# Two decode attentions on one core: A's second heads scored on the VectorE, one softmax step for four heads, and a gather dealt to 64 partitions

## The chip, the core and the metric

The kernel runs on one core of a Trainium2 chip: TensorE (PE), VectorE (DVE), ScalarE (ACT), GpSimd (POOL), a queue processor for transfers (SP), and 16 DMA engines. The metric is device time in microseconds (us), as the median of the runs.

## What is computed

One token `x` (448 numbers) goes through two attention blocks over cached keys and values, and a gate mixes the two results. Block A has 16 heads with a cache each; block B has 16 query heads on 8 caches, two heads to a cache.

```python
g = sigmoid((x * gate_w).sum(-1))
# A: H = 16; B: Hq = 16 on Hkv = 8;  Sk = 8192, Dh = 256, D = 448, all float32
q = (x @ wq).reshape(heads, Dh)
p = softmax(q @ k_cache^T * Dh ** -0.5)       # over 8192 keys, per head
o = p @ v_cache
block = o.reshape(heads * Dh) @ wo
out = g * block_A + (1 - g) * block_B
```

Every key and value is used once (in B for two heads), so some 430 MB are read for little arithmetic.

## The kernel before

**Sets and units.** The work is cut into eight sets (`NS`). Set `s` holds three units `(s, r)`: unit 2 is one B cache with its two heads, units 0 and 1 are two A heads. `UNITS = [2, 0, 1]` is their order. Each unit has four tiles (`NT`) of 2048 keys: a K tile and a V tile of 128 x 4096 numbers each. There are 96 tiles in all; the V tile of a step comes three steps (`LEAD`) after its K tile.

**The stream.** The host lays everything out in the order of use: K, V, query weights (`wq`), output weights (`wo`). `plan()` cuts this into 54 loads of up to 15,872 numbers per partition, and SP issues them one after another into a ring of three slots. A load can be issued when everything in the load three before it has been used. The last loads are cut finer; the last V tile comes in three pieces, and the last output weights come behind it in six.

**Scores.** In most units the PE multiplies K by the query (`scores`); DVE takes a minimum, ACT takes the exponential, DVE transposes it to weights `pr`. Units in `BY_ROW` go another way (`scores_by_row`): DVE multiplies the K tile in its slot by the query laid out over all partitions (`qa`), and reduces each row of 256 numbers to a score. Of a set's three units, before, only unit 0 is in `BY_ROW`. The PE then does `attend`: weights times V, summed over a unit's four tiles into the PSUM tile `o`. `take` folds that into `ob`.

**Softmax over tiles.** Each tile has its own minimum and sum (`st`). `gather(u)` lays them out in `gs`, `combine(u)` sums them on the PE and turns them into weights on one partition (`ew`, `es`, `z`, `wr`), `column(u)` turns them into a column `sel` by a PE product with `ones`, and `project_o(u)` multiplies `ob` by `sel`, into `ocs`. `emit_set` and `emit` multiply that by the output weights into `Y`. These steps are put off by `wait(n, f)`, which runs `f` after `n` more ticks; every finished K tile is a tick, and at the end the V tiles of the last three steps are.

**The gather by indirect DMA.** Set 4's query weights come partly by an indirect DMA that POOL issues (`side`). Only the partitions in `SIDE_ROWS` receive a row; `SIDE_SHARE` says how many of each group of eight partitions do. So the gather can put more bytes on some DMA engines than on others, while the stream loses the same weights on all partitions alike.

**Order on the engines.** The kernel is recorded once in program order (`Seq`), each engine executes its instructions in that order, and waits are derived from what overlaps. Nothing is reordered, so what is written earlier stands ahead in its engine's queue. The profile puts nearly all instructions at line 149, where they are emitted; they're told apart by their tiles.

Of the kernel before, what the change touches and what calls it, by code (L numbers as in the profile page):

```python
# [3 lines left out]
F32 = mybir.dt.float32  # L4
BF16 = mybir.dt.bfloat16
AF = mybir.ActivationFunctionType
OP = mybir.AluOpType
# [194 lines left out]
BY_ROW = {(s, 0) for s in range(NS)}  # L202
# [7 lines left out]
SIDE_SHARE = {0: 8, 2: 8, 7: 8, 8: 8, 15: 8, 4: 7, 1: 5, 3: 1, 6: 1, 10: 1}  # L210
# [3 lines left out]
SB, SA = 2 * DH, 64  # L214
# [56 lines left out]
def gated_decode_attention_kernel(  # L271
# [23 lines left out]
    zero = const.tile([P, P], BF16, name="zero")  # L295
# [29 lines left out]
    rows4 = const.tile([P, 4], F32, name="rows4")  # L325
# [6 lines left out]
    in4 = const.tile([P, 2, NG], F32, name="in4")  # L332
    nc.vector.tensor_copy(in4[:, 0, :], rows4)
# [6 lines left out]
    cols = const.tile([P, NT, NG, NT], F32, name="cols")  # L340
    nc.vector.memset(cols, 0.0)
    for t in range(NT):
        nc.vector.tensor_copy(cols[:, t, :, t], in4[:, 1, :])

    spread32 = const.tile([2 * BLK, P], F32, name="spread32")
    nc.vector.memset(spread32, 0.0)
    nc.vector.memset(spread32[BLK:BLK + 1, :], 1.0)

    QB = {}
    for par in range(2):  # L350
        for r in (r for r in range(3) if (par, r) not in BY_ROW or (par + 2, r) not in BY_ROW):
            QB[par, r] = const.tile([P, 2, 64], F32, name=f"qb{par}{r}")
            nc.vector.memset(QB[par, r], 0.0)

    xz = const.tile([P, KF + 2, BLK], F32, name="xz")
    nc.vector.memset(xz, 0.0)
# [15 lines left out]
    gate = const.tile([1, 2], F32, name="gate")  # L374

    def clear(t, n):
        nc.tensor.matmul(t[:, :n], zero, zero[:, None, :n // 4].to_broadcast([P, 4, n // 4]), start=True, stop=False, skip_group_check=True)
# [10 lines left out]
    def prepare(gw):  # L388
        clear(YY[0], D)
        gp = ps_s.tile([1, 1], F32, name="sm")  # L390
        for c in range(KF + 1):
            nc.tensor.matmul(gp, xz[:, c, 0:1], gw[:, c:c + 1], start=(c == 0), stop=(c == KF))
# [3 lines left out]
        nc.vector.reciprocal(gate[:, 0:1], ge)  # L396
        nc.vector.tensor_scalar(gate[:, 1:2], gate[:, 0:1], -1.0, 1.0, op0=OP.mult, op1=OP.add)
# [5 lines left out]
    def project(s, c0, w):  # L403

        if c0 == 0:
            QR[s] = ps_s.tile([2 * BLK, 2 * DH], F32, name="sm")
        q = QR[s]
        for j in range(w.shape[1]):
            a, c = divmod(c0 + j, KF)
            for a in (a,) if a < 2 else (0, 1):  # L410
                c = c if c0 + j < 2 * KF else KF
                nc.tensor.matmul(q[BLK * a:BLK * (a + 1), :], xz[:, c if c < KF else KF + a, :], w[:, j, :],
                                 start=(c == 0), stop=(c == KF), skip_group_check=True)
        if c0 + w.shape[1] == 2 * KF + 1:
            copy_out(s, q)
# [5 lines left out]
    def project_side(s, view, far):  # L421

        q = ps_s.tile([2 * BLK, 2 * DH], F32, name="sm")
        near = view[:, :KF * SREST].rearrange("p (c n) -> p c n", c=KF)
        rest = view[:, KF * SREST:]
        for a in range(2):
            nc.tensor.matmul(q[BLK * a:BLK * (a + 1), :], xz[:, KF + a, :], rest, start=True, stop=False,
                             skip_group_check=True)
        for c in range(KF):
            nc.tensor.matmul(q[BLK:2 * BLK, SA:], xz[:, c, :], near[:, c, :], start=False, stop=(c == KF - 1),  # L430
                             skip_group_check=True)
        for c in range(SC8):
            at = c * (SB + SA)
            nc.tensor.matmul(q[0:1, :], x8[:, c:c + 1], far[:, at:at + SB], start=False, stop=(c == SC8 - 1),
                             skip_group_check=True)
            nc.tensor.matmul(q[BLK:BLK + 1, :SA], x8[:, c:c + 1], far[:, at + SB:at + SB + SA], start=False,
                             stop=(c == SC8 - 1), skip_group_check=True)
        copy_out(s, q)

    def spread(s):  # L440
# [7 lines left out]
        for r, a, h, M in ((2, 0, 0, 2), (0, 1, 0, 1), (1, 1, 1, 1)):  # L448
            if (s, r) in BY_ROW:
                qa = ps_s.tile([P, DH], F32, name="sm")  # L450
                nc.tensor.matmul(qa, spread32, qr[:, h * DH:(h + 1) * DH], start=True, stop=True)
                QA[s, r] = small.tile([P, DH], F32, name="qa", bufs=1)
                nc.scalar.activation(QA[s, r], qa, AF.Copy, scale=-scale)
                continue
            nc.vector.tensor_scalar(QB[s % 2, r][:, :, BLK:BLK + M], qt[:, h:h + M, :, a].rearrange("p h e -> p e h"),
                                    -scale, None, op0=OP.mult)

    def scores(u, t, j0, kt):
# [6 lines left out]
        qb = QB[u[0] % 2, u[1]]  # L465
# [13 lines left out]
        pr = small.tile([P, NB * BLK], F32, name="pr", bufs=LEAD + 2)  # L479
# [5 lines left out]
    def scores_by_row(u, t, j0, kt):  # L485
# [10 lines left out]
        if j0 + n < ROWS:  # L496
# [9 lines left out]
        pr = small.tile([P, NB * BLK], F32, name="pr", bufs=LEAD + 2)[:, :ROWS * NG * NT].rearrange(  # L506
            "p (q c k) -> p q c k", c=NG * NT, k=2)
# [25 lines left out]
    def gather(u):  # L533

        M = heads(u)
        GS[u] = small.tile([P, 2, NG, NT, M], F32, name=f"gs{M}")
        st = ST[u][:, :, None, :].to_broadcast([P, 2, NG, NT])
        if u in BY_ROW:
            nc.vector.tensor_tensor(GS[u][:, :, :, :, 0], st, in4[:, :, :, None].to_broadcast([P, 2, NG, NT]), op=OP.mult)
        elif M == 1:  # L540
            nc.vector.tensor_tensor(GS[u][:, :, :, :, 0], st, POS[M][:, None].to_broadcast([P, 2, NG, NT]), op=OP.mult)
        else:
            pos = POS[M].rearrange("p g (t m) -> p g t m", m=M)
            for k in range(2):
                nc.vector.tensor_tensor(GS[u][:, k], ST[u][:, k, None, :, None].to_broadcast([P, NG, NT, M]), pos, op=OP.mult)

    def combine(u):

        M = heads(u)
        n = NG * NT  # L550
        gi = 1 if u[1] == 2 else 0
        T = ps_s.tile([1, 2, n * M], F32, name="sm")
        nc.tensor.matmul(T, ones, GS[u].rearrange("p k g t m -> p k (g t m)"), start=True, stop=True)
        mn = small.tile([1, 2], F32, name="mnr")
        z = small.tile([1, 2], F32, name="z")
        ew = small.tile([1, 2 * n], F32, name="ew")[:, :n * M]
        es = small.tile([1, 2 * n], F32, name="es")[:, :n * M]
        nc.vector.tensor_reduce(mn[:, :M], T[:, 0, :].rearrange("p (c m) -> p m c", m=M), axis=AX.X, op=OP.min)
        for m in range(M):
            nc.scalar.activation(ew[:, m::M], T[:, 0, m::M], AF.Exp, bias=mn[:, m:m + 1], scale=-1.0)  # L560
        nc.vector.tensor_tensor(es, ew, T[:, 1, :], op=OP.mult)
        nc.vector.tensor_reduce(z[:, :M], es.rearrange("p (c m) -> p m c", m=M), axis=AX.X, op=OP.add)
        rz = small.tile([1, 2], F32, name="rz")
        nc.vector.reciprocal(rz[:, :M], z[:, :M])
        WR[u] = small.tile([1, NG // M, n, M, 2], F32, name="wr")
        for m in range(M):
            nc.vector.tensor_scalar(
                WR[u][:, :, :, m, :], ew[:, None, m::M, None].to_broadcast([1, NG // M, n, 2]),
                rz[:, m:m + 1], gate[:, gi:gi + 1], op0=OP.mult, op1=OP.mult)

    def column(u):
        M = heads(u)
        cl = ps_s.tile([P, 1], F32, name="sm")
        nc.tensor.matmul(cl, WR.pop(u).rearrange("p c x m k -> p (c x m k)"), ones[:1, :], start=True, stop=True)
        SEL[u] = small.tile([P, 2], F32, name="sel")
        if M == 2:
            nc.vector.tensor_scalar(SEL[u], which, cl, None, op0=OP.mult)
        else:
            nc.scalar.activation(SEL[u][:, :1], cl, AF.Copy)

    def project_o(u):
        M = heads(u)
        oc = ps_s.tile([P, 2, 2], F32, name="sm")
        for e in range(2):
            nc.tensor.matmul(oc[:, e, :M], OB[u][:, e::2], SEL[u][:, :M], start=True, stop=True)
# [48 lines left out]
    def piece(kind, i, at, view):  # L634
# [17 lines left out]
        elif kind == "k":  # L652
# [54 lines left out]
    ys = const.tile([P, YN], F32, name="ys")  # L707
# [90 lines left out]
```

## Time and profile before

| what | before |
| --- | --- |
| median of 3 runs | 1005.64 us (1005.63 to 1005.69) |
| profiled execution | 1005.52 us, of it span 1003.6 us |
| PE busy | 586.4 us (58%) |
| DVE busy | 459.6 us (46%) |
| ACT busy | 94.1 us (9%) |
| stream, share of 16 DMA engines | 99.4%, 431.14 MB |
| gather | 0.89 MB |
| read from HBM | 433.20 MB, 432 GB/s over the span |
| mean granted TensorE clock | 0.774 |

A group's row gives engine, operation, output<-input, shape and count, then busy time in us and mean ns of one, then the idle time before them and what ended it. `slot` is a ring slot, `sc` the PE's scores, `sr` a by-row tile's scores, `o` the attended sums, `Y` the output; `sm` stands for all small PSUM products. A timeline row begins with its start and its duration in us; brackets hold the idle time before it. A float32 product appears as two matmuls and two weight loads (`PEld`). A windows row gives busy time per engine with counts, then the granted clock, the DMA share and GB/s.

### The profile page before, as it was taken

How to read it: one execution, taken by the hardware profiler on the slowest of the kernel's cores; microseconds unless marked ns; L12 is line 12 of the kernel's file. 1: busy time of each engine (PE TensorE's matmuls, PEld its weight loads, DVE VectorE, ACT ScalarE, POOL GpSimd, SP SyncE). 2: the span in 40 equal slices, each digit the busy share in tenths (PEclk: the TensorE clock that was granted, in tenths of full speed). 3: DMA queues.
4: the chain of work that ended last, by engine and by line, in shares of the span. 5: the costliest groups of instructions: out<-in, count | busy, mean ns of one | idle time of the engine just before them, and what ended most of it. 6: DMA issues, size and time to landing. Idle time of an engine off the chain costs nothing.

```text
span 1003.6 us, 7454 instructions
## 1 busy us (share of the span) xinstructions
PE 586.4 (58%) x3176; PEld 172.7 (17%) x3176; DVE 459.6 (46%) x651; ACT 94.1 (9%) x307; POOL 4.4 (0%) x20
## 2 busy tenths in 40 slices
PE   1855845665655654746747566445656747756457
PEld 0211211121111111212111121111211212111112
DVE  2386213961248521467213952257521585215852
ACT  0100100010100110001100011100110001100101
POOL 1000000000000000000000000000000000000000
PEclk9877777777787787777867777777776777877678
DMA  9999999999999999999999999999999999999998
GB/s 405 444 430 420 443 441 416 438 441 436 426 428 445 426 436 433 438 427 436 436 433 431 438 431 433 431 440 430 426 438 439 432 437 423 436 440 428 426 428 372
DMA packets 9545, 432.51 MB, mean 431 GB/s; under 512 B 1137, under 2 KB 1521, under 8 KB 2161
## 3 DMA queue, kind: packets, MB, share of 16 engines
q1 hardware_dynamic: 9364, 431.14, 99.4%
q0 software_dynamic: 144, 0.89, 0.2%
q8 instruction: 25, 0.41, 0.1%
q14 instruction: 8, 0.07, 0.0%
q10 hardware_dynamic: 4, 0.00, 0.0%
HBM read 433.20 MB, written 0.00 MB: 432 GB/s over the span
## 4 chain that ended last, share of the span: by engine, by line
DMA 71%; PE 15%; DVE 13%; ACT 1%; issue 0%; SPq 0%
DMA slot<-in_stream_dram 71%; PE o L149 7%; DVE sr L149 5%; PE sc L149 5%; DVE slot L149 5%; PE sm L149 2%; DVE pr L149 1%; DVE mn L149 1%; ACT px L149 1%; ACT pxr L149 0%; DVE st L149 0%; DVE ob L149 0%; PE Y L149 0%; ACT ew L149 0%; DVE mt L149 0%
## 5 line engine op out<-in xcount | busy, mean ns | idle before, releaser
L149 PE MATMUL o<-slot,pr 128*32 128x512 f32 (+1 forms) x1536 | 345.6, 764 | 206.1 <-DMA slot<-in_stream_dram 206.1
L149 PE MATMUL sc<-slot,qb 128*32 128x512 f32 x1024 | 195.8, 723 | 109.5 <-DMA slot<-in_stream_dram 109.4
L149 DVE TENSOR_REDUCE mn<-sc 128x1 f32<-128x512 f32 x64 | 44.2, 690 | 330.6 <-PE sc L149 301.2
L149 DVE TENSOR_TENSOR slot<-slot,qa 128x4096 f32<-128x4096 f32 (+6 forms) x39 | 142.4, 3652 | 44.9 <-DMA slot<-in_stream_dram 44.9
L149 PEld LDWEIGHTS o<-slot,pr 128*32 128x32 f32 (+1 forms) x1536 | 80.6, 143 | 382.8 <-DMA slot<-in_stream_dram 227.8
L149 DVE TENSOR_REDUCE sr<-slot 128x16 f32<-128x4096 f32 (+6 forms) x39 | 142.5, 3654 | 1.3
L149 PEld LDWEIGHTS sc<-slot,qb 128*32 128x32 f32 x1024 | 45.9, 130 | 226.9 <-DMA slot<-in_stream_dram 125.6
L149 ACT ACTIVATE px<-sc,st 128x512 f32<-128x512 f32 x64 | 44.0, 688 | 399.0 <-DVE st L149 399.0
L149 DVE STREAM_TRANSPOSE pr<-px 128x512 f32<-128x512 f32 x64 | 45.7, 713 | 54.1 <-ACT px L149 54.1
L149 PE MATMUL sm<-slot,xz 128*32 128x512 f32 (+2 forms) x130 | 44.9, 675 | 34.8 <-DVE xz L149 22.5
L149 ACT ACTIVATE pxr<-sr,st 128x16 f32<-128x16 f32 x32 | 9.8, 307 | 377.0 <-DVE st L149 377.0
L149 PE MATMUL sm<-sel,ob 128*128 128x1 f32 (+1 forms) x96 | 17.9, 290 | 34.9 <-DVE ob L149 34.9
L149 DVE SCALAR_TENSOR_TENSOR ob<-o,half,ob 128x256 f32<-128x256 f32 x24 | 11.4, 474 | 47.0 <-ACT ob L149 46.9
L149 PEld LDWEIGHTS sm<-sel,ob 128*128 128x128 f32 x96 | 15.8, 232 | 58.4 <-DVE ob L149 53.7
L149 PEld LDWEIGHTS sm<-slot,xz 128*32 128x32 f32 (+1 forms) x130 | 11.2, 127 | 65.1 <-issue 28.2
L149 DVE TENSOR_TENSOR pr<-pxr,cols 128x256 f32<-128x256 f32 x32 | 13.6, 425 | 15.0 <-ACT pxr L149 15.0
L149 PE MATMUL Y<-slot,ocs 128*1 128x448 f32 (+1 forms) x176 | 17.4, 459 | 3.8 <-DMA slot<-in_stream_dram 3.8
L149 ACT ACTIVATE ob<-o,half 128x256 f32<-128x256 f32 x24 | 11.3, 470 | 43.3 <-PE o L149 43.3
L149 PE MATMUL sm<-ones,wr 1*128 1x1 f32 x48 | 10.1, 277 | 7.4 <-DVE wr L149 7.2
L149 PE MATMUL sm<-px,spread 64*128 64x256 f32 x16 | 6.6, 497 | 13.1 <-DVE es L149 13.1
L149 PEld LDWEIGHTS sm<-ones,wr 1*128 1x128 f32 x48 | 8.0, 208 | 32.7 <-issue 18.8
L149 ACT ACTIVATION_READ_ACCUMULATOR px<-sc,st 128x1 f32 x64 | 12.4, 193 | 0.0
(69 smaller groups left out, 150.2 us busy)
## 6 DMA issues: line engine op xcount, KB each, us to landing
slot<-in_stream_dram SPq DMA_DIRECT2D x47, 7936.0 KB, 42.1
slot<-in_stream_dram SPq DMA_DIRECT2D x1, 7944.0 KB, 21.4
slot<-in_stream_dram SPq DMA_DIRECT2D x1, 7840.0 KB, 46.0
slot<-in_stream_dram SPq DMA_DIRECT2D x1, 7776.0 KB, 48.6
slot<-in_stream_dram SPq DMA_DIRECT2D x1, 5792.0 KB, 41.4
slot<-in_stream_dram SPq DMA_DIRECT2D x1, 5376.0 KB, 35.1
slot<-in_stream_dram SPq DMA_DIRECT2D x2, 2048.0 KB, 33.5
slot<-in_stream_dram SPq DMA_DIRECT2D x1, 2816.0 KB, 31.3
```

What stands on the lines that cost most here:

```text
L149: ins = getattr(engine, method)(*args, **kw)
```

## The change

- **By row:** unit 1 joins `BY_ROW` in sets 0 to 6; in the last set it stays on the PE. Both A heads of a set get their query laid out by one product and one copy (`both`).
- **One softmax step:** `gather` fills one `gs` for the whole set, and `combine(s)` and `column(s)` run once per set, over four heads, after the last K tile of unit 1. The projections of units 2 and 0 come after that. In the last set these run at the tick of the second to last V tile.
- **Merged products:** the rest rows of `wq` for both blocks are one product instead of two; the gate's sum is reduced on DVE ahead of one product instead of four; several constant tiles become views of one.
- **Gather:** 64 rows of 16,896 bytes instead of 55 of 16,128; the stream's part of set 4's weights shrinks from 1856 to 1472 numbers per partition.
- **Buffers:** five `pr` tiles become four, with eight smaller `prr` beside them for by-row tiles.

```diff
-BY_ROW = {(s, 0) for s in range(NS)}
+BY_ROW = {(s, r) for s in range(NS) for r in (0, 1) if (s, r) != (NS - 1, 1)}
...
-SIDE_SHARE = {0: 8, 2: 8, 7: 8, 8: 8, 15: 8, 4: 7, 1: 5, 3: 1, 6: 1, 10: 1}
+SIDE_SHARE = {0: 8, 2: 8, 7: 8, 8: 8, 15: 8, 4: 7, 1: 5, 5: 3, 13: 3, 14: 3, 3: 2, 10: 1}
...
-SB, SA = 2 * DH, 64
+SB, SA = 2 * DH, 192
...
+        qa = ps_s.tile([P, 2 * DH], F32, name="sm")
+        nc.tensor.matmul(qa, rows4[:2 * BLK, 1:2].to_broadcast([2 * BLK, P]), qr, start=True, stop=True)
+        both = small.tile([P, 2 * DH], F32, name="qa")
+        nc.scalar.activation(both, qa, AF.Copy, scale=-scale)
...
-    def combine(u):
+    def combine(s):
...
+        T = ps_s.tile([1, 2, NG, n], F32, name="sm")
+        nc.tensor.matmul(T, ones, GS.pop(s).rearrange("p k h g t -> p (k h g t)"), start=True, stop=True)
...
+        nc.vector.tensor_reduce(mn, T[:, 0], axis=AX.X, op=OP.min)
+        nc.vector.tensor_tensor(ew, T[:, 0], mn[:, :, None].to_broadcast([1, NG, n]), op=OP.subtract)
+        nc.scalar.activation(ew, ew, AF.Exp, scale=-1.0)
+        nc.vector.tensor_tensor(es, ew, T[:, 1], op=OP.mult)
+        nc.vector.tensor_reduce(z, es, axis=AX.X, op=OP.add)
+        nc.vector.reciprocal(z, z)
+        nc.vector.tensor_tensor(z, z, gate, op=OP.mult)
...
-    def column(u):
+    def column(s):
...
+        for k in range(3):
+            nc.tensor.matmul(cl[:, k:k + 1], WR[s][:, k], ones[:1, :], start=True, stop=True)
+        sel = small.tile([P, 2, 2], F32, name="sel")
+        nc.vector.tensor_scalar(sel[:, 0], which, cl[:, :1], None, op0=OP.mult)
+        nc.scalar.activation(sel[:, 1], cl[:, 1:], AF.Copy)
...
             if t == NT - 1:
                 gather(u)
-                wait(1, combine, u)
-                wait(2, column, u)
+                if u[1] == UNITS[-1]:
+                    s = u[0]
+                    wait(1, combine, s)
+                    wait(2, column, s)
+                    for r in UNITS[:2]:
+                        wait(2 if s == NS - 1 else 3, project_o, (s, r))
...
-                    if u != TILES[-1][0]:
+                    if u[1] == UNITS[-1] and u[0] < NS - 1:
                         wait(1, project_o, u)
```

The end of the PE's program, before (`gs` by `ones` is the softmax sum, `ones` by `wr` the column, `sel` by `ob` a projection, `o` an attended V tile):

```order
L149 MATMUL sm<-sel_110,ob_114 128x1 x2
L149 MATMUL o<-slot_51,pr_87 32x512 x8
L149 MATMUL o<-slot_51,pr_88 32x512 x8
L149 MATMUL sm<-gs_81_121,ones_49 1x32
L149 MATMUL o<-slot_51,pr_89 32x512 x8
L149 MATMUL sm<-ones_49,wr_109 128x1
L149 MATMUL o<-slot_52,pr_85 32x512 x8
L149 MATMUL sm<-sel_111,ob_115 128x1 x2
L149 MATMUL Y<-slot_52,ocs_117 1x112 x8
L149 MATMUL Y<-slot_52,ocs_119 1x112 x8
```

The same place after the change (the weights' row now lies in `px`):

```order
L149 MATMUL o<-slot_51,pr_81 32x512 x8
L149 MATMUL o<-slot_51,pr_82 32x512 x8
L149 MATMUL sm<-gs_85,ones_49 1x128
L149 MATMUL o<-slot_51,pr_83 32x512 x8
L149 MATMUL sm<-ones_49,px_61 128x1 x3
L149 MATMUL sm<-sel_110,ob_101 128x2 x2
L149 MATMUL sm<-sel_110,ob_102 128x1 x2
L149 MATMUL o<-slot_52,pr_84 32x512 x8
L149 MATMUL sm<-sel_110,ob_103 128x1 x2
L149 MATMUL Y<-slot_52,ocs_112 1x112 x8
L149 MATMUL Y<-slot_52,ocs_114 1x112 x8
```

Between the last two attended V tiles there was one column product; now there are three, and the projections of units 2 and 0 behind them.

On DVE, before, the passage from unit 0 to unit 1 in the fourth set. The first two rows are a by-row tile in its slot, then come its weights and its `gs`; the rows with `sc` are unit 1's first tile, scored on the PE:

```order
L149 TENSOR_TENSOR slot_50<-slot_50,qa_77 128x4096
L149 TENSOR_REDUCE sr_93<-slot_50 128x16
L149 TENSOR_REDUCE mn_84<-sr_93 128x1
L149 STREAM_TRANSPOSE mt_95<-mn_84 128x32
L149 TENSOR_REDUCE st_79<-mt_95 128x1
L149 TENSOR_TENSOR pr_87<-pxr_97,cols_67 128x256
L149 TENSOR_TENSOR gs_80_120<-st_79,in_18_66 128x32
L149 TENSOR_REDUCE mn_83<-sc 128x1
L149 TENSOR_TENSOR st_80<-mn_83,cap_11_59 128x1
L149 STREAM_TRANSPOSE pr_88<-px_60 128x8x2x32
```

The same passage after the change:

```order
L149 TENSOR_TENSOR slot_50<-slot_50,qa_71 128x4096
L149 TENSOR_REDUCE sr_87<-slot_50 128x16
L149 TENSOR_REDUCE mn_80<-sr_87 128x1
L149 STREAM_TRANSPOSE mt_89<-mn_80 128x32
L149 TENSOR_REDUCE st_75<-mt_89 128x1
L149 TENSOR_TENSOR prr_95<-pxr_91,empty_66 128x256
L149 TENSOR_TENSOR gs_85<-st_75,in_16_64 128x2x16
L149 TENSOR_TENSOR slot_51<-slot_51,qa_71 128x4096
L149 TENSOR_REDUCE sr_86<-slot_51 128x16
L149 TENSOR_REDUCE mn_79<-sr_86 128x1
```

Unit 1's first tile is now a second product in place and a second reduce over 4096 numbers, where a minimum over 512 and a transpose stood.

More of the change, by code (lines that the diff above doesn't have):

```diff
@@ L338, in gated_decode_attention_kernel @@
     nc.vector.tensor_reduce(in4[:, 1, :], block, axis=AX.X, op=OP.add)
[L340 to L358, printed above, removed]
+    empty = const.tile([P, NT * (NG * NT + 1) + 6 * 64 + (KF + 2) * BLK], F32, name="empty")
+    nc.vector.memset(empty, 0.0)
+    cols, qb = empty[:, :NT * (NG * NT + 1)], empty[:, NT * (NG * NT + 1):][:, :6 * 64]
+    QB = [qb[:, 2 * 64 * par:2 * 64 * (par + 1)].rearrange("p (e n) -> p e n", e=2) for par in range(3)]
+    xz = empty[:, NT * (NG * NT + 1) + 6 * 64:].rearrange("p (c n) -> p c n", n=BLK)
+    nc.vector.tensor_copy(cols.rearrange("p (t n) -> p t n", t=NT)[:, :, :NG * NT:NT],
+                          in4[:, 1, None, :].to_broadcast([P, NT, NG]))
+    cols = cols[:, :NT * NG * NT].rearrange("p (t g r) -> p t g r", t=NT, g=NG)
     x8 = const.tile([P, SC8], F32, name="x8")
@@ L389, in prepare @@
         clear(YY[0], D)
+        xw = const.tile([P, KF + 1], F32, name="xw")
+        nc.vector.tensor_tensor(xw, xz[:, :KF + 1, 0], gw, op=OP.mult)
+        xs = const.tile([P, 1], F32, name="xs")
+        nc.vector.tensor_reduce(xs, xw, axis=AX.X, op=OP.add)
         gp = ps_s.tile([1, 1], F32, name="sm")
-        for c in range(KF + 1):
-            nc.tensor.matmul(gp, xz[:, c, 0:1], gw[:, c:c + 1], start=(c == 0), stop=(c == KF))
+        nc.tensor.matmul(gp, xs, ones, start=True, stop=True)
         ge = const.tile([1, 1], F32, name="ge")
@@ L409, in project @@
             a, c = divmod(c0 + j, KF)
[L410 to L413, printed above, removed]
+            if a < 2:
+                nc.tensor.matmul(q[BLK * a:BLK * (a + 1), :], xz[:, c, :], w[:, j, :], start=(c == 0), stop=False,
+                                 skip_group_check=True)
+            else:
+                nc.tensor.matmul(q, xz[:, KF:KF + 2, :].rearrange("p c n -> p (c n)"), w[:, j, :], start=False, stop=True,
+                                 skip_group_check=True)
         if c0 + w.shape[1] == 2 * KF + 1:
@@ L425, in project_side @@
         rest = view[:, KF * SREST:]
-        for a in range(2):
-            nc.tensor.matmul(q[BLK * a:BLK * (a + 1), :], xz[:, KF + a, :], rest, start=True, stop=False,
-                             skip_group_check=True)
+        nc.tensor.matmul(q, xz[:, KF:KF + 2, :].rearrange("p c n -> p (c n)"), rest, start=True, stop=False,
+                         skip_group_check=True)
         for c in range(KF):
@@ L533, in gather @@
     def gather(u):
[L535 to L541, printed above, removed]
+        s, r = u
+        if r == UNITS[0]:
+            GS[s] = small.tile([P, 2, NG, NG, NT], F32, name="gs", bufs=1)
@@ L544, in gather @@
             for k in range(2):
-                nc.vector.tensor_tensor(GS[u][:, k], ST[u][:, k, None, :, None].to_broadcast([P, NG, NT, M]), pos, op=OP.mult)
-    def combine(u):
-        M = heads(u)
+                nc.vector.tensor_tensor(GS[s][:, k, :2], ST[u][:, k, None, None, :].to_broadcast([P, 2, NG, NT]),
+                                        POS[2].rearrange("p g (t m) -> p m g t", m=2), op=OP.mult)
+    def combine(s):
         n = NG * NT
[L551 to L569, printed above, removed]
@@ new lines, in combine @@
+        nc.vector.tensor_reduce(z, es, axis=AX.X, op=OP.add)
+        nc.vector.reciprocal(z, z)
+        nc.vector.tensor_tensor(z, z, gate, op=OP.mult)
+        WR[s] = small.tile([P, NB * BLK], F32, name="px")[:1, :3 * P].rearrange("p (k n) -> p k n", k=3)
+        for h in range(NG):
+            if h < 2:
+                w = WR[s][:, 0].rearrange("p (c x m k) -> p c x m k", x=n, m=2, k=2)[:, :, :, h, :]
+                nc.vector.tensor_scalar(w, ew[:, None, h, :, None].to_broadcast([1, 2, n, 2]), z[:, h:h + 1], None,
+                                        op0=OP.mult)
+            else:
+                w = WR[s][:, h - 1].rearrange("p (c x k) -> p c x k", x=n, k=2)
+                nc.scalar.activation(w, ew[:, None, h, :, None].to_broadcast([1, NG, n, 2]), AF.Copy, scale=z[:, h:h + 1])
@@ L581, in project_o @@
+    def column(s):
+        cl = ps_s.tile([P, 3], F32, name="sm")
+        for k in range(3):
[3 more added lines that the diff above has]
+        nc.scalar.activation(sel[:, 1], cl[:, 1:], AF.Copy)
+        SEL[s, 2], SEL[s, 0], SEL[s, 1] = sel[:, 0], sel[:, 1, :1], sel[:, 1, 1:]
     def project_o(u):
```

61 lines of the change are left out of this document (29 added, 32 removed).

## The prediction

> **What bounds the kernel now.** I read the page first, then the chain of waits in order of time, then the groups of instructions by form, and last the timeline of the end.
>
> ```profile
> span 1003.6 us, 7454 instructions
> PE 586.4 (58%) x3176; PEld 172.7 (17%) x3176; DVE 459.6 (46%) x651; ACT 94.1 (9%) x307; POOL 4.4 (0%) x20
> DMA  9999999999999999999999999999999999999998
> q1 hardware_dynamic: 9364, 431.14, 99.4%
> q0 software_dynamic: 144, 0.89, 0.2%
> q8 instruction: 25, 0.41, 0.1%
> DMA 71%; PE 15%; DVE 13%; ACT 1%; issue 0%; SPq 0%
> slot<-in_stream_dram SPq DMA_DIRECT2D x47, 7936.0 KB, 42.1
> ```
>
> The DMA engines are busy in every slice; the stream alone takes 99.4% of their span. No compute engine is over 58%. The stream costs 0.994 x 1003.6 / 431.14 = 2.31 us per MB, so a full load (15,872 numbers in each of 128 partitions, 8.13 MB) takes 18.8 us. It lands 42.1 us after its issue in the median; without its own 18.8 us, that leaves 23 us of loads ahead of it. The chain's PE and DVE shares are releases of slots, each followed by a DMA that had that queue before it; they aren't time in which the DMA stood still. So compute counts in two ways only: if a slot is freed so late that the queue runs dry, and after the last bytes.
>
> How near to dry by-row tiles bring it, the chain shows in the seventh set:
>
> ```profile
> 807.19 4.44 DVE slot L149
> 811.65 4.43 DVE sr L149
> 817.77 4.34 DVE slot L149
> 822.13 4.43 DVE sr L149
> 826.63 36.64 DMA slot<-in_stream_dram
> ```
>
> These are two by-row tiles, each a product in place and a reduce, 817.77 - 807.19 = 10.6 us apart. The slot is freed behind them, and the next load lands 36.6 us after it: 36.6 - 18.8 = 17.9 us were still queued.
>
> The end is the other place:
>
> ```profile
> 983.99 0.55 PEld L149 LDWEIGHTS sm<-sel,ob 128*128 128x128 f32 x4 [0.84 <-DVE ob L149]
> ...
> 987.31 1.92 PE L149 MATMUL o<-slot,pr 128*32 128x512 f32 x16 [0.83 <-DMA slot<-in_stream_dram]
> ...
> 989.05 0.22 PE L149 MATMUL sm<-gs,ones 128*1 128x32 f32 x2
> ...
> 992.15 3.48 PE L149 MATMUL o<-slot,pr 128*32 128x512 f32 x16 [2.88 <-DMA slot<-in_stream_dram]
> ...
> 995.56 0.29 PEld L149 LDWEIGHTS sm<-ones,wr 1*128 1x128 f32 x2 [1.50 <-issue]
> 995.56 0.38 PE L149 MATMUL sm<-ones,wr 1*128 1x1 f32 x2
> ...
> 995.87 2.25 PE L149 MATMUL o<-slot,pr 128*32 128x512 f32 x16
> 995.98 0.17 ACT L149 ACTIVATE sel<-sm 128x1 f32<-128x1 f32 x1 [6.20 <-PE sm L149]
> ...
> 997.07 0.14 PEld L149 LDWEIGHTS o<-slot,pr 128*32 128x32 f32 x4 [0.20 <-DMA slot<-in_stream_dram]
> ...
> 998.67 0.48 DVE L149 SCALAR_TENSOR_TENSOR ob<-o,half,ob 128x256 f32<-128x256 f32 x1 [7.96 <-ACT ob L149]
> 999.21 0.55 PEld L149 LDWEIGHTS sm<-sel,ob 128*128 128x128 f32 x4 [2.00 <-DVE ob L149]
> ...
> 999.77 1.55 PEld L149 LDWEIGHTS Y<-slot,ocs 128*1 128x1 f32 x60
> ...
> 1001.53 0.09 PEld L149 LDWEIGHTS Y<-slot,ocs 128*1 128x1 f32 x4 [0.20 <-DMA slot<-in_stream_dram]
> ...
> 1001.86 0.63 SPq L149 DMA_DIRECT2D out_dram<-ys  x2
> ```
>
> The V tiles of the last three steps are attended at 987.31, 992.15 and 995.87. The PE runs almost without a gap from 992.15; the last output weights make it wait just 0.20 us. So the PE's chain and the DMA end within 0.2 us of each other: work put between 992.15 and 999.77 shows in the time almost in full, while a stream that ended earlier would gain 0.2 us at the end itself and, by bringing the 992.15 landing forward, some more.
>
> **The change part by part. By-row tiles.** Seven sets times four tiles leave the PE for the DVE.
>
> ```profile
> L149 PE MATMUL sc<-slot,qb 128*32 128x512 f32 x1024 | 195.8, 723 | 109.5 <-DMA slot<-in_stream_dram 109.4
> L149 DVE TENSOR_REDUCE sr<-slot 128x16 f32<-128x4096 f32 x25 | 110.5, 4420 | 0.9
> L149 DVE TENSOR_TENSOR slot<-slot,qa 128x4096 f32<-128x4096 f32 x25 | 110.4, 4417 | 25.6 <-DMA slot<-in_stream_dram 25.6
> L149 DVE STREAM_TRANSPOSE pr<-px 128x512 f32<-128x512 f32 x64 | 45.7, 713 | 54.1 <-ACT px L149 54.1
> L149 DVE TENSOR_REDUCE mn<-sc 128x1 f32<-128x512 f32 x64 | 44.2, 690 | 330.6 <-PE sc L149 301.2
> L149 DVE TENSOR_TENSOR pr<-pxr,cols 128x256 f32<-128x256 f32 x32 | 13.6, 425 | 15.0 <-ACT pxr L149 15.0
> L149 DVE TENSOR_TENSOR st<-mn,cap 128x1 f32<-128x1 f32 x64 | 10.2, 160 | 2.2
> L149 DVE STREAM_TRANSPOSE mt<-mn 128x32 f32<-128x32 f32 x32 | 6.8, 211 | 1.1
> L149 DVE TENSOR_REDUCE st<-mt 128x1 f32<-128x32 f32 x32 | 6.0, 186 | 1.1
> L149 DVE TENSOR_REDUCE mn<-sr 128x1 f32<-128x16 f32 x32 | 5.4, 170 | 1.1
> L149 DVE TENSOR_SCALAR sel<-which,sm 128x2 f32<-128x2 f32 x8 | 1.8, 228 | 0.0
> ```
>
> Off the PE: 28 x 16 x (195.8/1024) = 86 us. Onto the DVE: 28 x (4.42 + 4.42 + 0.43 + 0.21 + 0.19 + 0.17, less 0.71 + 0.69 + 0.16) = +232 us, so near 690 us of busy time. Does that still keep up? A set has eight by-row tiles, in a stretch of eight K tiles, eight V tiles, one query-weight and one output-weight block: 16 x 4096 + 2 x 3584 = 72,704 numbers, 4.58 loads or 86 us. The DVE needs 8 x 10.6 = 85 us, and about 3 for the rest: it ends the stretch some 2 to 5 us behind. Four B tiles follow, 39 us of stream for 4 x 1.56 = 6 us of DVE and its waits, so each set starts afresh. A load holds at most two by-row tiles and a little, so its slot is freed at most 21 + 5 = 26 us after it landed. The queue would be dry 2 x 18.8 = 37.6 us after. The margin falls from 17.9 to about 11 us and stays a margin: this part costs **0**. The work that covers it is the two loads in flight; with the cover gone, every us over is a us lost. The PE's products saved are worth 0 too, since PE's idle time is spent waiting for the stream.
>
> **Copies, merged products, start.** Zeroed tiles, the broadcast weights, the gate's product and the merged query products lie before the first products, while the first load is still under way, or among PE work that has gaps: **0**. Were all their cover gone, they'd cost tenths of a us.
>
> **The gather.** The stream loses 384 x 512 B = 0.197 MB; the gather goes from 55 rows of 16,128 B to 64 of 16,896 B, +0.194 MB. The order of the PE falls from 1589 listed products to 1336; a listed product is two matmuls and two weight loads in the profile, so about 1,010 instructions go. At 0.41 MB / 6,352 = 65 B each that is 0.065 MB of instruction packets, four of the 25. In sum -0.07 MB, or -0.16 us if dealt evenly. But what counts is the latest of the sixteen engines. Each loses 12.3 KB of stream, 0.45 us at 27 KB/us (431.14 MB over 16 engines in 998 us). If, as the table seems to mean, each of its entries is one engine, those that keep no rows gain the whole 0.45 us, and the three that go from none to three rows (50.7 KB) are 1.4 us later, unless the saved instruction packets were theirs. Bounds -0.45 and +1.4; I take **-0.3 us**, since nothing forces the worse end.
>
> **One softmax step for four heads.** In sets 1 to 7 its steps wait for the fourth head's gather, with B's tiles running under them: 0. In the last set they end up in the tail. Before, two of the three units had been projected earlier (the second at 983.99); only one column product stood between the last two V tiles. Now three column products, the wait for sel, and two projections stand there, and the last V tile queues behind them on the PE. In turn: two more column products at 995.87 - 995.56 = 0.31 each, +0.62. From the start of the last column product to sel takes 0.38 + 0.04 (995.56 to 995.98), then the DVE's sel 0.23 and 0.06 until the PE goes on (ob ends at 999.15, the load starts at 999.21): 0.71, of which 0.31 is the product's own slot, so +0.40. Two projections at 999.77 - 999.21 = 0.56, +1.11. Together 2.13 us. The last V tile now comes after all its pieces: 1.92 instead of 2.25, -0.33. The output products no longer wait: -0.20. **+1.6 us**; the bounds are +0.6 (only the two column products count, as if the rest went under attended products) and +2.1 (no wait saved). The bigger sum over four heads itself starts behind the product at 989.05 and has until 995.56: hidden; it would need over 6 us to show.
>
> The sum on the profiled execution: 1005.52 + 0 - 0.3 + 1.6 = 1006.8 us (its span, 1003.6, and 1.9 around it, unchanged). The median of the runs is 0.12 above that execution: **1006.9 us**, +0.13%. About 0.2%, or 2.0 us, is what a measurement of this kernel can tell from no change, so this counts as the same.
>
> **The rivals.** *The tail runs at full clock.*
>
> ```profile
> 990.00:995.00 5.00, 2.85 (x16) 0.59 (x16) 0.64 (x3) 0.00 (x0) 0.00 (x0) 0.69 0.96 404
> 995.00:1000.00 5.00, 3.91 (x38) 1.60 (x38) 0.48 (x1) 0.76 (x3) 0.00 (x0) 0.97 1.02 414
> ```
>
> In the windows the granted clock is 0.69 where the tile at 992.15 ran, which took 3.48 us where the same shape took 1.92 at 987.31. The PE had stood for under 3 us before it. Without that slow stretch the chain is 1.56 us earlier: the last V tile starts at 995.87 + 2.13 - 1.56 - 0.3 = 996.1 and, its last piece landing by 996.8, ends at about 998.1 as before. Then the added steps are free, and the stream's -0.3 is left: **1005.4 us**. For it: the slow stretch costs just what the addition costs. Against: the idle time before stays nearly the same, so the clock should fall again. The Trainium skill, "TensorE: Matmul & The Clock Gate", Part 1: The HAM clock gate, says that the clock is set by activity in free-running windows of about 3.4 us; by that, the slow stretch may fall elsewhere from run to run, and runs could differ by up to this 1.56 us. The three runs of before agree within 0.06 us, but there the DMA hides a faster PE.
>
> *The DVE starves the queue* (the other side). At the end of each set the PE's sum over four heads waits for the gather behind the eighth by-row tile; V tiles and the next scores stand behind it on the PE, and slots behind those. If that brings a release past 37 us after its landing, where I have 26, the DMA stops once a set. At 2 us over, seven sets give 14 us: **1021 us**. For it: 85 + 3 us of DVE in 86 us of stream. Against: 11 us of margin, and PE work that is light there.
>
> *The rows are dealt worse*: the end of the stream +1.4 instead of -0.3, tail as forecast: **1008.6 us**. For it: a third of the rows' moves go to engines that had none. Against: fetches do move with the PE's program.
>
> *The redealing does nothing*: no -0.3; 1007.2, inside the forecast.
>
> **How the numbers follow.** Forecast 0.52 (1005.8 to 1007.7: the tail's bounds with -0.45 and with 0 for the stream), full clock 0.26, dealt worse 0.10, starved 0.08, a gain that I don't see 0.04. The range 1005.0 to 1008.8 holds the first three; it leaves out starvation and the unseen gain. Faster by over 0.2% (under 1003.6) needs 2 us of stream to vanish, which no term gives: 0.04. Slower by over 0.2% (above 1007.65): starved 0.08, most of dealt worse 0.08, the top of the forecast 0.05: 0.21. The same: 0.75.
>
> **What would show it.** Right: stream share still over 99%, DMA 9 in all slices; DVE near 690 us, PE near 500; in the timeline of the end three column products and two projections between the last two attended V tiles, and a last weight load that no longer waits for DMA. Wrong: a slice below 9 before the end (starved); a load that lands under 25 us after its issue in a by-row stretch; the last output weights still waited for (full clock, or dealt worse, told apart by the landing before 992); a span under 1001.6 or over 1006.

## The result, and the profile after

The changed kernel takes 1008.13 us in the median of 22 runs (1005.30 to 1012.33), the kernel before 1005.71 in 22 runs beside them (1005.52 to 1006.14). The ratio is 1.0025, with a 95% interval of 1.0013 to 1.0036: slower by 2.4 us, or 0.25%. That is just over the 0.2% that the prediction took as the bound, and the interval reaches to both sides of it. The runs of before lie within 0.6 us, those of after are spread over 7 us; half of them are under 1007.5. The profiled execution of after, with 1009.82 us, is above its median.

The page after, in the parts that answer to those shown of before:

```profile
span 1008.0 us, 6461 instructions
...
PE 532.7 (53%) x2670; PEld 156.4 (16%) x2670; DVE 679.2 (67%) x669; ACT 83.2 (8%) x291; POOL 4.3 (0%) x20
...
DMA  9999999999999999999999999999999999999997
...
q1 hardware_dynamic: 9364, 430.95, 98.9%
q0 software_dynamic: 144, 1.08, 0.3%
q8 instruction: 21, 0.34, 0.1%
...
DMA 63%; DVE 24%; PE 11%; ACT 1%; issue 1%; SPq 0%
...
slot<-in_stream_dram SPq DMA_DIRECT2D x47, 7936.0 KB, 40.0
```

The DVE has 220 us more to do, and the stream is still in every slice but the last: 40.0 us from issue to landing in the median, against 42.1. The shortest time of a full load in the chain of waits comes after a by-row tile and the first piece of the next:

```profile
480.64 4.34 DVE slot L149
485.01 4.43 DVE sr L149
490.99 1.15 DVE slot L149
492.16 1.23 DVE sr L149
493.41 34.01 DMA slot<-in_stream_dram
```

34.0 - 18.8 = 15.2 us were still queued when the slot came free. So no load in this chain came near to running dry. The timeline of the end has it all:

```profile
989.38 0.38 PE L149 MATMUL sm<-gs,ones 128*1 128x128 f32 x2
...
992.50 3.36 PE L149 MATMUL o<-slot,pr 128*32 128x512 f32 x16 [2.74 <-DMA slot<-in_stream_dram]
...
995.80 0.82 PE L149 MATMUL sm<-ones,px 1*128 1x1 f32 x6
996.66 0.23 DVE L149 TENSOR_SCALAR sel<-which,sm 128x2 f32<-128x2 f32 x1 [4.68 <-PE sm L149]
...
996.95 1.10 PE L149 MATMUL sm<-sel,ob 128*128 128x2 f32 x8 [0.33 <-DVE sel L149]
...
997.98 2.82 PE L149 MATMUL o<-slot,pr 128*32 128x512 f32 x16
...
1001.89 1.01 PE L149 MATMUL sm<-sel,ob 128*128 128x1 f32 x4 [1.09 <-DVE ob L149]
...
1002.83 3.08 PE L149 MATMUL Y<-slot,ocs 128*1 128x112 f32 x64
...
1006.25 0.62 SPq L149 DMA_DIRECT2D out_dram<-px  x2
```

The last V tile starts at 997.98 instead of 995.87, +2.11 us: the V tile ahead of it starts 0.35 later (992.50, 992.15), it takes 0.11 less until the first column product, and from there to the last V tile it's 2.18 instead of 0.31, +1.87, for the column products and projections. The last V tile then takes 2.82 us instead of 2.25, the last projection's step 0.94 (1001.89 to 1002.83) instead of 0.56, and from there to the store 3.42 instead of 2.09. The four make 2.11 + 0.57 + 0.38 + 1.33 = 4.4 us, which is the whole difference of the spans, 1008.0 - 1003.6. No weight load waits for DMA at the end any more: the PE's chain ends the kernel, not the stream.

The windows show why the second half of that chain was slow. The columns are PE, weight loads, DVE, ACT and POOL busy, then the granted clock, the DMA share and GB/s. First after, then before. In both traces every stretch at one clock lasts 3.41 us or a whole multiple of it, and the windows are cut on that grid:

```profile
992.04:995.45 3.41, 2.94 (x16) 0.59 (x16) 0.00 (x0) 0.10 (x1) 0.00 (x0) 0.50 1.00 414
995.45:998.86 3.41, 3.08 (x26) 2.04 (x26) 0.23 (x1) 0.52 (x3) 0.00 (x0) 1.00 1.03 420
998.86:1002.28 3.42, 2.33 (x14) 0.59 (x7) 0.48 (x1) 0.47 (x1) 0.00 (x0) 0.50 0.51 190
1002.28:1005.69 3.41, 3.41 (x67) 2.67 (x67) 0.00 (x0) 0.17 (x1) 0.00 (x0) 0.50 0.02 5
```

```profile
991.93:995.34 3.41, 3.19 (x16) 0.59 (x16) 0.00 (x0) 0.00 (x0) 0.00 (x0) 0.50 0.99 412
995.34:998.76 3.42, 2.78 (x22) 0.83 (x18) 0.09 (x1) 0.65 (x2) 0.00 (x0) 1.00 1.03 418
998.76:1002.17 3.41, 2.67 (x68) 2.03 (x68) 0.90 (x3) 0.17 (x1) 0.00 (x0) 1.00 0.65 246
```

Both kernels run the second to last V tile at half clock and get full clock behind it. In the next stretch the changed kernel's PE is busy for 3.08 us, more than the 2.78 of before, but with weight loads (2.04 us of it beside 0.83) and products of one or two columns. After that it is back at 0.50 and stays there nearly to the end; the kernel before stays at 1.00. A fall after so much busy time is out of the ordinary: in the whole trace of before, cut on the same grid, 54 stretches at full clock were followed by half clock, and none of them has more than 1.77 us of busy PE.

### The profile page after: what moved, and what is told of

Read it like the earlier page. It is cut to its first block, busy times and chain, and to the rows that moved or that the text cites. A ratio compares the mean times of both kernels' runs of the same rounds, so it can differ in the third digit from the quotient of the medians.

```text
span 1008.0 us, 6461 instructions
## 1 busy us (share of the span) xinstructions
PE 532.7 (53%) x2670; PEld 156.4 (16%) x2670; DVE 679.2 (67%) x669; ACT 83.2 (8%) x291; POOL 4.3 (0%) x20
## 3 DMA queue, kind: packets, MB, share of 16 engines
q1 hardware_dynamic: 9364, 430.95, 98.9%
## 4 chain that ended last, share of the span: by engine, by line
DMA 63%; DVE 24%; PE 11%; ACT 1%; issue 1%; SPq 0%
DMA slot<-in_stream_dram 63%; DVE sr L149 10%; DVE slot L149 10%; PE o L149 5%; PE sc L149 3%; PE sm L149 3%; DVE prr L149 1%; ACT pxr L149 1%; DVE mn L149 1%; DVE st L149 0%; DVE mt L149 0%; DVE ob L149 0%; ACT px L149 0%; PE Y L149 0%; DVE px L149 0%
## 5 line engine op out<-in xcount | busy, mean ns | idle before, releaser
L149 DVE TENSOR_TENSOR slot<-slot,qa 128x4096 f32<-128x4096 f32 (+7 forms) x74 | 267.2, 3611 | 58.5 <-DMA slot<-in_stream_dram 58.4
L149 PE MATMUL o<-slot,prr 128*32 128x512 f32 x960 | 179.5, 828 | 176.7 <-DMA slot<-in_stream_dram 176.6
L149 DVE TENSOR_REDUCE sr<-slot 128x16 f32<-128x4096 f32 (+7 forms) x74 | 267.3, 3613 | 2.5
L149 PE MATMUL o<-slot,pr 128*64 128x512 f32 (+1 forms) x576 | 163.2, 742 | 126.2 <-DMA slot<-in_stream_dram 126.2
L149 PE MATMUL sc<-slot,empty 128*32 128x512 f32 x576 | 107.8, 748 | 85.6 <-DMA slot<-in_stream_dram 85.5
L149 PEld LDWEIGHTS o<-slot,prr 128*32 128x32 f32 x960 | 38.5, 140 | 288.4 <-DMA slot<-in_stream_dram 201.5
L149 PEld LDWEIGHTS o<-slot,pr 128*64 128x64 f32 (+1 forms) x576 | 44.7, 164 | 232.9 <-DMA slot<-in_stream_dram 140.0
L149 PE MATMUL sm<-slot,empty 128*32 128x512 f32 (+2 forms) x106 | 44.3, 697 | 41.4 <-DVE empty L149 22.8
L149 PEld LDWEIGHTS sc<-slot,empty 128*32 128x32 f32 x576 | 26.0, 133 | 150.9 <-DMA slot<-in_stream_dram 94.6
L149 DVE TENSOR_TENSOR prr<-pxr,empty 128x256 f32<-128x256 f32 x60 | 25.5, 425 | 28.0 <-ACT pxr L149 28.0
```

The costliest lines, as they stand in the source:

```text
L149: ins = getattr(engine, method)(*args, **kw)
```

## The experiments

The theory to test: the time is lost in the tail alone, partly as queue (the small products before the last V tile), partly as half-clock stretches which those products bring on and which fall differently from run to run. Against it stood two rivals from the prediction: the DVE starving the stream (rival 1), and the gather's rows dealt worse (rival 2).

**Softmax steps by unit again (unit_steps).** All of the change stays but this. The variant's softmax steps share scratch tiles with a set's query row, which they overwrite in places, so some values differ; the amount of work doesn't. The edit, shortened to its schedule:

```diff
-    wait(1, combine, s); wait(2, column, s)      # once per set, then two projections
+    wait(1, combine, u); wait(2, column, u)      # once per unit, projections as before
```

> The changed kernel, but softmax steps (gather, combine, column, projection) by unit as before; by-row tiles, merged products and the new gather stay. Theory (the tail): the loss is the small products that stand between the last two V tiles, about 2.1 us of queue, and half-clock stretches there that fall differently from run to run; so here the time goes back to 1005.2 to 1005.8 us, and all runs lie within 0.7 us. Rival 1 (DVE starves the stream in some runs): the by-row tiles are still there, so runs still spread over 1005 to 1012 with a median near 1008. Rival 2 (rows dealt worse): the same as rival 1, since the gather is still the new one.

1006.26 us (1006.10 to 1006.74, 11 runs) beside 1005.86 of before: ratio 1.0004 (0.9995 to 1.0013). The spread of 7 us is gone with by-row tiles and gather in place, which leaves neither rival room as its cause. The median is 0.5 us above what the theory gave, and 0.4 over before. The gather explains at most a part of that: by_row_alone, below, has these softmax steps with the old gather and is still 0.3 over the runs of before beside it.

**The one softmax step alone (before_one_step).** The kernel before, with `gather`, `combine`, `column` and their schedule from after.

> The kernel before with nothing of the change but the one softmax step per set. Theory (the tail): median 1007 to 1009 us, single runs from 1005.3 to over 1010. Rivals 1 (DVE) and 2 (dealing): 1005.7 us with a spread of 0.6, since neither by-row tiles nor gather are changed.

1009.68 us (1009.63 to 1011.13, 5 runs), ratio 1.0040 (1.0026 to 1.0054), with neither a by-row tile nor a gathered row changed. That is more than the whole change costs. Its tail, in the timeline and in the windows:

```profile
992.49 2.46 PE L149 MATMUL o<-slot,pr 128*32 128x512 f32 x16 [2.73 <-DMA slot<-in_stream_dram]
...
994.87 1.44 PE L149 MATMUL sm<-ones,px 1*128 1x1 f32 x6
...
996.64 1.87 PE L149 MATMUL sm<-sel,ob 128*128 128x2 f32 x8 [0.33 <-DVE sel L149]
...
998.43 3.64 PE L149 MATMUL o<-slot,pr 128*32 128x512 f32 x16
...
1003.18 1.01 PE L149 MATMUL sm<-sel,ob 128*128 128x1 f32 x4 [1.11 <-DVE ob L149]
...
1004.13 3.17 PE L149 MATMUL Y<-slot,ocs 128*1 128x112 f32 x64
```

```profile
993.74:997.15 3.41, 3.08 (x17) 1.87 (x9) 0.23 (x1) 0.17 (x1) 0.00 (x0) 0.50 1.01 414
997.15:1000.57 3.42, 3.42 (x19) 1.86 (x22) 0.00 (x0) 0.34 (x2) 0.00 (x0) 0.50 1.01 402
1000.57:1003.98 3.41, 2.30 (x12) 0.80 (x4) 0.48 (x1) 0.47 (x1) 0.00 (x0) 0.50 0.11 38
1003.98:1007.40 3.42, 3.31 (x66) 2.27 (x65) 0.07 (x1) 0.17 (x1) 0.00 (x0) 0.50 0.00 0
```

In this execution (1011.08 us) half clock began in the middle of the second to last V tile and lasted to the output products: 1.44 and 1.87 us where the changed kernel's profile has 0.82 and 1.10, and 3.64 where it has 2.82.

**The same steps one V tile earlier (early_steps).** The changed kernel, with one line moved so that in the last set the sum runs before the third to last V tile, and column products and projections before the second to last.

```diff
-                if i >= len(TILES) - LEAD:
+                if i >= len(TILES) - LEAD - 1:
                     tick()
```

> The changed kernel with the last set's softmax steps one V tile earlier: the sum over four heads before the third to last V tile's end of queue, column products and two projections before the second to last V tile, where the PE stands for about 3 us and waits for the stream. Theory (the tail): 1005.2 to 1005.8 us, runs within 0.8 us; the last V tile starts right behind the one before it. Rivals 1 and 2: median near 1008, spread 1005 to 1012, as the changed kernel.

1006.18 us (1005.43 to 1006.48, 11 runs), ratio 1.0002 (0.9993 to 1.0011). Every instruction of the one softmax step is still there, but the column products and two projections now lie in the 3 us in which the PE waits for the stream:

```profile
989.23 0.82 PE L149 MATMUL sm<-ones,px 1*128 1x1 f32 x6
...
990.38 1.10 PE L149 MATMUL sm<-sel,ob 128*128 128x2 f32 x8 [0.33 <-DVE sel L149]
...
992.24 6.00 PE L149 MATMUL o<-slot,pr 128*32 128x512 f32 x32 [0.75 <-DMA slot<-in_stream_dram]
```

The last two V tiles are one row now, with no small products between them. So the price was the place, not the steps. The median is again 0.4 us over the theory's range; the execution profiled, with 1005.43 us, is the lowest of the eleven.

**The old gather with it (early_old_deal), and the new gather alone (before_new_deal).** Two lines each, in opposite directions; here those of early_old_deal:

```diff
-SIDE_SHARE = {0: 8, 2: 8, 7: 8, 8: 8, 15: 8, 4: 7, 1: 5, 5: 3, 13: 3, 14: 3, 3: 2, 10: 1}
+SIDE_SHARE = {0: 8, 2: 8, 7: 8, 8: 8, 15: 8, 4: 7, 1: 5, 3: 1, 6: 1, 10: 1}
...
-SB, SA = 2 * DH, 192
+SB, SA = 2 * DH, 64
```

> As early_steps, and the gather as before (55 rows of 16,128 bytes). Measures the gather by itself against early_steps. Theory: the dealing moves the stream's end by under 0.5 us either way, so this lies within 0.5 us of early_steps; forecast by my sum: 0.3 us later than early_steps. Rival 2 (new rows dealt worse): this at 1005.7 and early_steps some us above it.

> The kernel before with the new gather alone (64 rows of 16,896 bytes, dealt as after the change), with the old program on the PE and so its old instruction packets. Theory: by bytes, the engines that go from none to three rows end 1.4 us later, so 1006.5 to 1007.3 us; if the spread between the engines hides part of it, no less than 1006. Rival (the dealing does nothing): 1005.8.

With the old gather early_steps falls from 1006.18 to 1005.57 us (1005.50 to 1006.10, 11 runs; ratio to before 0.9997, 0.9988 to 1.0006). The new gather put into the kernel before raises it from 1005.76 to 1006.58 us (1006.40 to 1007.06, 11 runs; ratio 1.0008, 0.9999 to 1.0017): every one of its runs is over every one of the 26 of before (highest 1006.28). So in these two pairs the new gather costs 0.6 to 0.8 us. In before_new_deal it shows at the stream's end:

```profile
1002.54 0.09 PEld L149 LDWEIGHTS Y<-slot,ocs 128*1 128x1 f32 x4 [0.20 <-DMA slot<-in_stream_dram]
```

The last output weights are there 1.0 us later than before (1001.53, with the same 0.20 us of waiting). The timelines of the other pair can't show it: the executions profiled are the lowest run of early_steps and the second highest of early_old_deal. A third pair shows less: unit_steps and by_row_alone, which differ in the gather and in some buffers, are 0.4 and 0.3 us over the runs of before beside each. My expectation for early_old_deal had the sign wrong, and the 0.6 us is over its bound of 0.5; the one for before_new_deal held.

**Equal PE time, two shapes (before_small, before_wide).** The kernel before, with added products between the last two V tiles whose results aren't used.

```diff
+                if i == len(TILES) - 2:                     # before_small: one column each
+                    for e in range(8):
+                        nc.tensor.matmul(oc[:, e % 2, :1], OB[NS - 1, 0][:, e % 2::2], SEL[NS - 1, 0][:, :1], ...)
...
+                    for e in range(9):                      # before_wide: 512 columns each
+                        nc.tensor.matmul(sc[32 * (e % 4):32 * (e % 4 + 1), :], QB[1, 1][:, e % 2, 32:64], PR[u, t], ...)
```

> The kernel before, with eight more products of one column (128 x 128 weights each, results unused) between the last two V tiles: about 2.2 us of PE time at full clock. Nothing else of the change. Theory (clock): products of one column keep the PE busy in the records but count for little in what sets the clock, so a half-clock stretch follows them; median 1007 to 1010 us, single runs over 1009. Rival (queue alone): the added 2.2 us less 0.5 of waits saved, all runs at 1007.2 to 1007.8.

> The kernel before, with nine more products of 512 columns at the same place (results unused): also about 2.2 us of PE time at full clock. Theory (clock): these keep the clock up, so only the queue shows: 1007.0 to 1008.0 us, no run over 1009 but where the half-clock stretch that is there already covers them as well (then up to 2 us more). Rival (queue alone): as before_small, within 0.3 us of it. Second rival (any added work lowers the clock): as before_small, with runs over 1009.

before_small: 1010.29 us (1006.21 to 1012.78, 6 runs), ratio 1.0041 (1.0025 to 1.0056). before_wide: 1008.09 us (1006.55 to 1009.29, 8 runs), ratio 1.0022 (1.0012 to 1.0032). The same 2.2 us of PE at full clock cost 4.5 us in one shape and 2.3 in the other, and the small products alone bring the spread of the changed kernel. That speaks for the clock and against the queue alone. before_wide came out 0.1 us over the range I had given, and one run passed 1009. The windows of before_small, then of before_wide:

```profile
993.61:997.02 3.41, 3.41 (x18) 1.51 (x10) 0.00 (x0) 0.17 (x1) 0.00 (x0) 0.50 1.01 413
997.02:1000.44 3.42, 3.42 (x18) 2.90 (x21) 0.00 (x0) 0.00 (x0) 0.00 (x0) 0.50 1.02 406
1000.44:1003.85 3.41, 2.93 (x16) 0.40 (x8) 0.00 (x0) 0.41 (x1) 0.00 (x0) 0.50 0.17 59
```

```profile
993.63:997.04 3.41, 3.41 (x18) 0.90 (x14) 0.00 (x0) 0.17 (x1) 0.00 (x0) 0.50 1.00 410
997.04:1000.46 3.42, 3.42 (x30) 0.87 (x22) 0.00 (x0) 0.00 (x0) 0.00 (x0) 1.00 1.02 407
```

In both the PE is busy without a gap from 993.6 on, at half clock. With products of 512 columns the full clock is back after 3.4 us; with products of one column it is back neither after 3.4 us nor after 6.8 us.

**Work added ahead of the tail (after_warm).** The changed kernel, with ten products of 512 columns (results unused) while the PE waits for the second to last V tile.

```diff
+                    if s == NS - 1:
+                        wait(1, warm, u, t)      # ten 128x32 by 128x512 products into a free bank
```

> The changed kernel, with ten products of 512 columns (results unused) in the 3 us in which the PE waits for the second to last V tile, about 2.4 us. Theory (clock): the first half-clock stretch, on that V tile, goes, though the small products behind it may still bring on another: median 1006 to 1007.5 us, at least 0.7 us under the changed kernel's 1008.1, with work added. Rival (queue alone): the same as the changed kernel or later.

1007.00 us (1005.41 to 1009.21, 11 runs), ratio 1.0015 (1.0006 to 1.0024): 1.1 us under the changed kernel's 1008.13, with more work. This was as expected, but it is a hint and not a proof: the two were measured on different occasions, and the interval of the ratio overlaps that of the change (1.0013 to 1.0036). None of the eleven runs is over 1010, where six of the changed kernel's 22 were. In the windows of the profile the second to last V tile runs at full clock, and the small products behind it are followed by half clock again, which fits the spread that's left:

```profile
991.22:994.64 3.42, 3.42 (x34) 1.88 (x28) 1.54 (x8) 0.95 (x3) 0.00 (x0) 1.00 0.98 408
994.64:998.05 3.41, 3.08 (x25) 1.92 (x22) 0.23 (x1) 0.52 (x3) 0.00 (x0) 1.00 1.02 417
998.05:1001.46 3.41, 2.84 (x16) 0.44 (x8) 0.01 (x1) 0.47 (x1) 0.00 (x0) 0.50 0.79 303
```

**By-row tiles and merged products alone (by_row_alone).** The changed kernel with softmax steps by unit, the gather as before, and six `prr` tiles instead of eight for room.

> The changed kernel with softmax steps by unit and the gather as before; the second heads by row and the merged products are left of the change (six prr tiles instead of eight, to make room). Theory: 28 more by-row tiles cost nothing, since two loads are always queued: 1005.5 to 1006.0 us, runs within 0.8 us. Rival 1 (DVE starves the stream): over 1006.5 us, or runs spread by more than 2 us.

1006.08 us (1005.97 to 1006.37, 11 runs), ratio 1.0003 (0.9994 to 1.0012): 0.3 us over before, 0.08 over the range I gave, with a spread of 0.4. No starvation. In its profile the last output weights are waited for:

```profile
1002.46 0.09 PEld L149 LDWEIGHTS Y<-slot,ocs 128*1 128x1 f32 x4 [0.21 <-DMA slot<-in_stream_dram]
```

So the stream's end is later there too, by 0.9 us in this execution, the highest of its eleven, and with the old gather. What shifts it wasn't isolated. The count of instruction packets isn't enough to explain it: it is 21, as in early_old_deal, which has the old gather as well and isn't slower than before.

**A better version (before_early, early_old_deal_2).** The kernel before with the one line of early_steps, and early_old_deal again, on one chip.

> The kernel before with the last unit's softmax steps one V tile earlier, and nothing else. Theory: 0.3 us less on the PE's chain between the last two V tiles, where the stream's end is within 0.2 us of it: 1005.3 to 1005.8 us, at most 0.3 us under the kernel before; a better version if it shows. Rival (the end is the stream's alone): no change, 1005.8.

> early_old_deal again, beside the two others on one chip: the fastest version so far. Theory: 1005.4 to 1005.8 us and within 0.3 us of by_row_alone and before_early, since all three end with the stream.

before_early: 1005.79 us (1005.55 to 1006.42, 11 runs), ratio 0.9999 (0.9990 to 1.0008), against 1005.79: no change, as its rival said. early_old_deal_2: 1005.68 us (1005.53 to 1005.92, 11 runs), the same ratio and interval. The latter beats the changed kernel by 2.5 us and equals the one before; no version here is faster than the kernel before by an amount that could be told.

## Why the prediction was right, and where it wasn't

**By-row tiles at 0: right.** DVE 679 us (forecast near 690), a margin of 15 us (forecast about 11; the 17.9 it started from is 17.8), all DMA slices at 9 but the last. early_old_deal has all the by-row tiles and takes 1005.57 and, run again, 1005.68 us, no more than before; by_row_alone and unit_steps show no starvation either, and that rival falls. PE fell to 533 us, not to near 500, at a mean granted clock of 0.744 instead of 0.774; it cost nothing.

**The tail: the queue right, the clock missed.** The place and the products were as forecast, and their price nearly: +1.87 us between the column product and the last V tile, against 2.13. The step that failed is the one after it: "The last V tile now comes after all its pieces: 1.92 instead of 2.25, -0.33", and the unchanged price of what follows. They assumed full clock behind the small products. In the profile the last V tile took 2.82 us, the last projection's step 0.38 more than before and the output products' 1.33 more. The term was +1.6 with an upper bound of +2.1. In the profile it is 4.4 less the 0.35 of the later landing, or 4.0. In the median of the runs it is about 2.1: after is 2.4 us over the runs of before beside it, and early_steps, which differs from it in the place of these steps alone, 0.3.

**The sum, by the medians.** 1008.13 is 1.2 us over the forecast of 1006.9. About 0.5 of it is the tail, 2.1 against 1.6. About 0.6 is the stream's end, where early_steps is 0.3 over before and the sum had -0.3. The forecast's own bounds, 1005.8 to 1007.7, missed the median by 0.4. That it fell into the wider range, to 1008.8, is partly luck: the range reached so far for the sake of rows dealt 1.4 us worse with an unchanged tail, and no run shows that.

**Full clock in the tail: half right.** The lowest runs, 1005.30 to 1005.86 (six of 22), lie about where that rival had them, 1005.4. Which windows they had isn't known, as none of them was profiled; their mean clock over the span, 0.750 to 0.753, doesn't tell it, since runs of 1011.64 and 1011.98 us have 0.752. I weighed a faster tail and not a slower one, and the profile of after has two half-clock stretches in its tail, from 992.04 and from 998.86. The rule that the prediction cites, of free-running windows in the Trainium skill, "TensorE: Matmul & The Clock Gate", Part 1: The HAM clock gate, allows a second one as well as the first. A range to 1008.8 held the median, but only half of the runs.

**The gather at -0.3: wrong in sign.** "I take -0.3 us, since nothing forces the worse end": the two pairs of runs show +0.6 and +0.8, inside the bounds of -0.45 and +1.4. The prediction's other argument, by the bytes of each engine (its +1.4), had the sign right, and the four saved instruction packets (25 to 21, as forecast) didn't make room. That the three engines with new rows are what ends late is argued and not shown: rows, their size and the dealing changed together, and no profile here shows the engines one by one.

**The chances and the signs.** By the bound of 0.2% the median is slower (1.0025), which had 0.21 against 0.75 for the same; the interval takes in both. Of the signs set beforehand, the three column products, the two projections and the last weight load that no longer waits came as said. The stream's share was 98.9%, not over 99%, as the tail grew longer, and the span, 1008.0 us, passed the 1006 that was to count as wrong.

What stays open: why the one softmax step costs 3.8 us in the kernel before and 2.1 in the changed one. Both have runs that fit half clock in most of the tail; the share of such runs differs, and 5 runs of one are few.

## What to carry to other kernels

In a kernel that the stream bounds, as long as slots come free in time, the engines' time counts only at the end, and there a small product between the last two tiles is paid almost in full: put such steps where the PE waits for the stream, one tile earlier. Price a tail at half clock as well as at full, and look at the spread of the runs, not just at the median. When bytes are dealt to single DMA engines, price the one that gets most as well as the mean: here the total hardly changed, and the time rose by 0.6 to 0.8 us in two pairs of runs.

## What was not expected of the hardware

A PE that is busy without a gap isn't thereby kept at full clock. Through 6.8 us of unbroken PE work, the first 3.4 with some and the next with mostly products of one column, the granted clock stayed at 0.50 (before_small); with products of 512 columns it was 1.00 after 3.4 us (before_wide). At full clock, 3.08 us of busy PE in 3.41 us, of it 2.04 with weight loads, were followed by half clock (after), and 2.78 us with 0.83 of weight loads by full clock (before). The Trainium skill, "TensorE: Matmul & The Clock Gate", Part 1: The HAM clock gate, says that PE activity in such windows releases the throttle. These runs fit columns streamed as that activity better than time busy. One stretch speaks against weight loads as what brings the fall: from 29.37 us on, the kernel before has 1.99 us of them in 3.41 us, beside about 1 us of products of two columns and more of 256 to 512, and the full clock went on. No experiment here separates the two.
